# The first expert group's transposes ahead of the fourth half batch's counts, the third group's w1 ahead of its rows, and the fourth batch of x loaded in five pieces

## The chip, the cores and the metric

The kernel runs on one core of one Trainium2 chip. The metric is device time in microseconds (us), lower is better; a comparison is made of several timed executions of each kernel on the same chip. One execution is also recorded by the hardware profiler, and all rows below are from that one.

## What is computed

The input is a batch of 8 sequences of 2496 rows and 256 columns. The reference takes a two-dimensional Fourier transform of each, keeps the real part, and sends the 19968 rows that result through a mixture of 8 experts, one expert per row:

```python
X = np.fft.fft(x, axis=1)
X = np.fft.fft(X, axis=2)
x = X.real.reshape(B * S, D)            # 19968 x 256
logits = x @ w_gate                     # 256 x 8
expert_idx = np.argmax(logits, axis=1)
gate_w = softmax(logits)[arange, expert_idx]
h = np.maximum(xe @ w1[e], 0.0)         # rows of expert e, 256 -> 1024
out[mask] = gate_w[mask, None] * (h @ w2[e])   # 1024 -> 256
```

## The kernel before

**Two halves that overlap.** The transform goes in 16 half batches, called units: the even and the odd part (par 0 and 1) of each of the 8 batches. For one unit VectorE (DVE) folds the loaded x (`fold_w`, `fold_fg`, `fold_z`, `fold_h`, lines 474 to 505), TensorE (PE) multiplies along the sequence (L356, in two quarters q = 0 and 1) and along the columns (`along_d`, L682 to L691), and `route_a` and `route_b` (L529 to L631) find each row's expert, count the rows of each expert (two small matmuls against a triangle and ones, L586 and L587, the *counts*), and scatter the rows by POOL's indirect DMA into a table in DRAM named `bucket` (L617), sorted by expert. The numbers of the rows (L527) are put beside the data by POOL.

**Groups.** The experts' half takes rows from `bucket` in groups. The first 12 groups are of 256 rows of one expert. Which expert and which rows a group has is not known ahead: `first_row` makes a table for the first two groups once units 0 and 1 are counted, and `group_rows` with `table_row` (L923, L1012) makes the next table, for the groups from the third on, once units 0 to 3 are. SP (the engine that issues loads) copies a table into a row, `row<-tab` (L918 and L1022), and reads registers from it (`reg`, L1039). For each group SP loads the rows (`load_rows`, `xr`, L1053), and w1 and w2 of the expert in four pieces each (`load_w`, L1084). A load of rows waits until the scatters of the units that its table covers have landed.

**One group.** PE transposes the rows (`xpose`, L1100), ACT writes a rounded copy `xh` (L1106) and DVE the rest `xl` (L1107). Each w1 piece is split likewise into `wah` (ACT, L1120) and `wal` (DVE, L1121), each w2 piece into the two halves of `wb` (L1135, L1136). For each of four pieces p the first GEMM is 12 matmuls of 256 columns (L1154 to L1156); ACT's relu makes `hh` (L1159) and DVE the rest `hl` (L1160); the second GEMM is 12 matmuls (L1187 to L1190) that read `hh`, `hl` and `wb`, placed two pieces behind the first (`LAG = 2`). `put` scales and writes the result (L1208 to L1211).

**What sets the order.** Inside `start()` (units 0 to 3) the order on PE, DVE and ACT is that of the code (`manual_schedule`). After it a scheduler orders each engine's instructions by its own estimates, beginning from the order in which the code emits them: the main loop takes `next(todo)` for a step of the transform and `next(moe)` for a step of the experts, in a ratio set by `THIRD` and `LEAD`. SP takes its loads in the order in which they are emitted (`after("sp")`), so an instruction that waits holds back all that stand behind it. The PSUM tiles `psH` (4 buffers) are shared by both halves. `load_x(3)` loads batch 3 in two halves of 1.3 MB, `x` having two buffers, so that it waits until PE has read batch 1.

Of the kernel before, what the change touches and what calls it, by code (L numbers as in the profile page):

```python
# [33 lines left out]
WARM = 18  # L34
EARLY = 2
LEAD = 4
THIRD = 26
THREE = 7
FIRST = 8
FSTEPS, AHEAD = 28, 6  # L40
AHEAD_IDS = 3
# [15 lines left out]
SURE = PAIRED + len(ENDING)  # L57
# [151 lines left out]
def fft2_then_moe(ctx: ExitStack, tc: tile.TileContext, i: dict, out: bass.AP):  # L209
# [33 lines left out]
    def load_x(b):  # L243
        x = ff.tile([P, 4, 5, 256], F32, name="x")
        src = i["xin"][b]
        for h in range(2):
            with after("sp"):
                ins = nc.sync.dma_start(out=x[:, 2 * h : 2 * h + 2], in_=src[:, 2 * h : 2 * h + 2])
        xs_of[b] = x
        ch["sp"] = ins.ins  # L250

    slots = ((0, 2), (2, 4), (4, 5))

# [220 lines left out]
    def fold_w(b, sl):  # L474

        x, s = xs_of[b], slice(*sl)
        ch["w"] = nc.vector.tensor_add(x[:, 0::2, s], x[:, 0::2, s], x[:, 1::2, s])
        yield

    def fold_fg(b, sl):  # L480
# [48 lines left out]
    def route_a(b, par, rb, st, fine=False):  # L529
# [44 lines left out]

        if not fine:
            gate()
        if 2 * b + par >= AHEAD_IDS:
            put_ids(rb, b, par)
        st["lg"], st["ohf"], st["ohb"], st["rest"] = lg3, ohf, ohb, (gate, mirror)
        yield  # L580

    def route_b(b, par, rb, st, fine=False):
# [59 lines left out]
    def fft_steps():  # L642
# [88 lines left out]
        def start():  # L731
# [77 lines left out]
            pc()  # L809
            run(tab)  # L810
            qc()
            fb = chain(fold_z(1, 1), fold_batch(2))
            next(fb)
            for _ in along_d(2, (0, 2, 4)):
# [15 lines left out]
                next(fb)  # L830
            st, rb = {}, cols.pop(3)
            run(route_a(1, 1, rb, st, True))
            rb3 = route_b(1, 1, rb, st, True)
            next(rb3)
            next(fb)
            run(rb3)
            return fb

        with ordered():
            fb = start()  # L840
        ch["done"] = 2
        yield
        load_x(3)
        yield
        _, w, g0, count = cuts()[1]
        for _ in group_rows(w, g0, count):
            yield
            next(fb, None)
            yield
        ch["row", 4] = table_row()  # L850
        yield
# [3 lines left out]
        for u, (b, par) in enumerate(units):  # L855
            if u < 4:
                continue
            if par == 0 and 2 < b < B - 1:
                load_x(b + 1)
            three = par and u >= THREE  # L860
            for q in range(2):
                if three:
                    ch["z", u, q] = split_odd(b, q)
                    yield
                if u == THREE - 1:
                    odd_table(1 - q)
                along_s(u, q)
                yield
                if q == 0 and late is not None:
                    yield from late  # L870
            if par == 0:
                yield from fold_z(b, 1)
            elif b + 1 < B:
                yield from fold_batch(b + 1)
            yield from along_d(u)
            late = route(u)
            if u + 1 in [n for n, _, _ in SEGS]:
                yield from late
                late = None
                ch["done"] = u + 1  # L880
# [204 lines left out]
        ch["sp"] = ins.ins  # L1085

    def xpose(g, part):

        xr, n = ch[g]["xr"], tall[g]
        if n < 4 and part:  # L1090
# [6 lines left out]
        for q in range(0 if blocked(g) else 4 if n > 1 else 2):  # L1097
            k, a = (part, q) if n == 4 else divmod(q, n)
            c = (T1, T2)[k]
            nc.tensor.transpose(out=hp[:, q * P : (q + 1) * P], in_=xr[:, a, c : c + P], identity=ident)  # L1100
        if n == 1:
            ch[g]["x"] = mo.tile([P, D], F32, name="ys", bufs=4)
            hi = lo = nc.scalar.copy(ch[g]["x"], hp[:, 0 : 2 * P]).ins
        else:
            xh, xl = (v[:, part] for v in ch[g]["x"])
            hi = nc.scalar.copy(xh, hp).ins  # L1106
            lo = nc.vector.tensor_sub(xl, hp, xh.bitcast(F32)).ins  # L1107
        if part == 0 and not blocked(g):
            gt = mo.tile([P, 4, 2], F32, name="gt", bufs=8)
            with tc.issue_after(hi):  # L1110
                nc.scalar.copy(gt[:, 0:n, 0], xr[:, 0:n, GATE])
            with tc.issue_after(lo):
                nc.vector.tensor_copy(gt[:, 0:n, 1].bitcast(I32), xr[:, 0:n, TID].bitcast(I32))
            ch[g, "gt"] = gt

    def split(src, name):
        hi = mo.tile([P, 512], F32R, name=name + "h")
# [105 lines left out]
    def moe_steps(g0, g1):  # L1223
# [9 lines left out]
        if g0 == 0:  # L1233
            load_rows(g0)
            yield g0
        for part in range(2):
            xpose(g0, part)
        if tall[g0] > 1:
            split1(g0, 0)
        for n in range(len(units) + LAG):  # L1240
            if n < len(units):
                g, p, fs = units[n]
                more, half = g + 1 < g1, tall[g] == 1
                if p == 0 and fs[0] == 0 and more:
                    load_rows(g + 1)
                    w_regs(g + 1)
                    if not half:
                        load_w(g + 1, w1r, "w1", 0)
                if p < 3 and fs[0] == 0 and not half:
                    split1(g, p + 1)  # L1250
                    if more:
                        load_w(g + 1, w1r, "w1", p + 1)
                elif p == 3 and more and not half:
                    xpose(g + 1, fs[0])
                    if fs == (0, 1):
# [29 lines left out]
    for n in sorted({s[0] for s in segs}):  # L1285
        todo = fft_until(n)
        if moe is not None:
# [3 lines left out]
            nm = sum(4 * tall[g] for g in span)  # L1291
            if ch["at"] == 0:
                nf = THIRD
                next(moe)
                for _ in range(LEAD):
                    next(todo, None)
                nf -= LEAD
# [21 lines left out]
        for g in have:  # L1319
            rows_of[g] = row, n  # L1320
        if moe is None:
            moe, ch["at"] = moe_steps(0, SURE), 0
    for _ in moe:
        pass
    total = nc.values_load(row[0:1, 3:4], min_val=0, max_val=KINDS.count("H"))
# [24 lines left out]
```

## Time and profile before

| what | value |
|---|---|
| timed executions, median of 3 | 1188.2 us (1183.52 to 1189.18) |
| the profiled execution | 1166.6 us, of which 1164.5 us are the span from first to last instruction |
| mean granted TensorE clock over the span | 0.968 of full speed |
| busy share of the span | PE 93%, DVE 70%, ACT 52%, POOL 30% |

The profiled execution is 1.8% below the median of the timed ones. Times in the rows count from the start of the span. PE's clock has two levels, shown as 1.00 (2.4 GHz) and 0.50 (1.2 GHz). "Idle before" an instruction is put down to the one that ended the wait; "issue" means that the profile shows nothing that it waited for, "remote" that a semaphore came which the profile can't put to an instruction.

### The profile page before, as it was taken

The page shows a single profiled execution, that of the slowest core. Times are in us where ns is not written, and L with a number is a line of the kernel's source. Part 1 is how long each engine was busy: PE and PEld are TensorE (multiplying, and loading weights), DVE is VectorE, ACT ScalarE, POOL GpSimd, SP SyncE. Part 2 cuts the span into 40 slices and gives each one's busy share as a digit, 9 for nine tenths or more (in the row PEclk, how much of TensorE's full clock was granted, in tenths as well). Part 3 has the DMA queues.
Part 4 walks back from the last instruction along what each step waited for, and adds up shares of the span by engine and source line. Part 5 has one row for each costly group of instructions (what it writes and reads, how often), then busy time and mean ns, then how long its engine had stood idle before and what let it go on. Part 6 is the DMA issues. An engine that isn't in the chain of part 4 may idle for free.

```text
span 1164.5 us, 21457 instructions
## 1 busy us (share of the span) xinstructions
PE 1085.4 (93%) x6229; PEld 926.0 (80%) x6229; DVE 820.5 (70%) x1810; ACT 601.2 (52%) x1375; POOL 353.7 (30%) x348
## 2 busy tenths in 40 slices
PE   8759999999897998997988999999999999999996
PEld 4548998998676787786766888888888888899995
DVE  7678877966887878574666666666666665667774
ACT  2245575765444555353443545555555555556664
POOL 1744524524445142424424112111211211211111
PEclk9979998999998999898989999999999999999999
DMA  9665676557473574451524434453343413455510
GB/s 353 218 229 174 206 244 197 162 142 255 105 223 132 130 228 123 134 133 67 133 59 124 131 64 118 110 129 70 102 115 64 113 38 55 155 157 192 172 47 26
DMA packets 202485, 163.88 MB, mean 141 GB/s; under 512 B 148786, under 2 KB 151827, under 8 KB 200440
## 3 DMA queue, kind: packets, MB, share of 16 engines
q1 hardware_dynamic: 186292, 116.84, 37.7%
q0 software_dynamic: 15776, 45.43, 10.2%
q8 instruction: 51, 0.84, 0.3%
q14 instruction: 74, 0.61, 0.2%
q10 hardware_dynamic: 292, 0.17, 0.1%
HBM read 162.21 MB, written 44.94 MB: 178 GB/s over the span
## 4 chain that ended last, share of the span: by engine, by line
PE 83%; issue 6%; DVE 5%; DMA 2%; another core or an unknown queue 2%; ACT 2%; SPq 0%; POOL 0%; POOLq 0%; DVEq 0%; ACTq 0%
PE psY L1197 21%; PE psH L1154 12%; PE psH L1155 12%; PE psH L1156 12%; PE psY L1198 10%; PE psH L356 2%; PE psY L1187 2%; PE psY L1190 2%; PE psY L1189 2%; PE psH L691 2%; PE psH L690 1%; DMA x<-xin 1%; PE psH L401 1%; PE psH L1100 1%
## 5 line engine op out<-in xcount | busy, mean ns | idle before, releaser
L1197 PE MATMUL psY<-wb,hh 128*128 128x512 f32 x1088 | 405.3, 405 | 15.9 <-DVE ys L1210 12.8
L1211 POOL DMA_INDIRECT out<-ys,gt x160 | 173.6, 1085 | 565.9 <-DVE ys L1210 465.2
L1198 PE MATMUL psY<-wb,hl 128*128 128x256 f32 x1088 | 307.5, 283 | 0.5 <-DVE hl L1160 0.5
L1154 PE MATMUL psH<-xh,wah 128*128 128x512 f32 (+1 forms) x784 | 283.6, 362 | 5.0 <-issue 3.4
L1155 PE MATMUL psH<-xl,wah 128*128 128x512 f32 (+1 forms) x784 | 278.3, 355 | 3.1 <-DVE wb L1136 1.2
L1156 PE MATMUL psH<-xh,wal 128*128 128x512 f32 (+1 forms) x784 | 275.3, 351 | 0.9 <-issue 0.9
L1160 DVE SCALAR_TENSOR_TENSOR hl<-psH,hh 128x512 fp32r<-128x512 f32 (+1 forms) x328 | 220.9, 673 | 60.8 <-ACT hh L1159 47.2
L1197 PEld LDWEIGHTS psY<-wb,hh 128*128 128x128 f32 x1088 | 207.1, 190 | 68.6 <-DVE ys L1210 14.8
L1159 ACT ACTIVATE hh<-psH 128x512 fp32r<-128x512 f32 (+1 forms) x328 | 192.3, 586 | 69.6 <-PE psH L1156 51.7
L1120 ACT CAST wah<-w1r 128x512 fp32r<-128x512 f32 x196 | 121.8, 622 | 205.3 <-PE psH L1155 153.6
L1121 DVE TENSOR_TENSOR wal<-w1r,wah 128x512 fp32r<-128x512 f32 x196 | 135.3, 690 | 130.1 <-ACT wah L1120 92.8
L617 POOL DMA_INDIRECT bucket<-rb,di x160 | 172.0, 1075 | 150.6 <-issue 69.0
L1198 PEld LDWEIGHTS psY<-wb,hl 128*128 128x128 f32 x1088 | 207.7, 191 | 9.7 <-DVE hl L1160 1.5
L1136 DVE TENSOR_TENSOR wb<-w2r,wb 128x512 fp32r<-128x512 f32 x212 | 145.4, 686 | 53.2 <-ACT wb L1135 28.3
L1135 ACT CAST wb<-w2r 128x512 fp32r<-128x512 f32 x212 | 132.5, 625 | 85.1 <-PE psY L1198 48.5
L1154 PEld LDWEIGHTS psH<-xh,wah 128*128 128x128 f32 x784 | 151.3, 193 | 31.7 <-issue 7.6
L1156 PEld LDWEIGHTS psH<-xh,wal 128*128 128x128 f32 x784 | 151.5, 193 | 23.1 <-issue 2.4
L1155 PEld LDWEIGHTS psH<-xl,wah 128*128 128x128 f32 x784 | 151.4, 193 | 13.7 <-issue 2.1
L1208 ACT ACTIVATE ys<-psY,gt 128x256 f32<-128x256 f32 x160 | 65.4, 478 | 12.9 <-PE psY L1190 4.7
L1106 ACT CAST xh<-psH 128x512 fp32r<-128x512 f32 x78 | 45.9, 588 | 44.9 <-DVE psH L1096 42.6
L1107 DVE TENSOR_TENSOR xl<-psH,xh 128x512 fp32r<-128x512 f32 x78 | 53.6, 688 | 14.7 <-ACT xh L1106 13.1
L1210 DVE SCALAR_TENSOR_TENSOR ys<-psY,gt,ys 128x256 f32<-128x256 f32 x136 | 57.5, 476 | 5.4 <-ACT ys L1208 2.7
(217 smaller groups left out, 1108.2 us busy)
## 6 DMA issues: line engine op xcount, KB each, us to landing
w1r<-w SPq DMA_DIRECT2D x212, 256.0 KB
w2r<-w SPq DMA_DIRECT2D x212, 256.0 KB
x<-xin SPq DMA_DIRECT2D x12, 1280.0 KB
xr<-bucket SPq DMA_DIRECT2D x232, 64.0 KB
xr<-bucket SPq DMA_DIRECT2D x20, 266.0 KB
x<-xin SPq DMA_DIRECT2D x3, 1024.0 KB
bucket<-rb,di POOLq DMA_INDIRECT x160
out<-ys,gt POOLq DMA_INDIRECT x160
```

What stands on the lines that cost most here:

```text
L617: ins = nc.gpsimd.indirect_dma_start(out=bucket[:, :], out_offset=IndirectOffsetOnAxis(ap=di[:, n : n + 1].bitcast(U32), axis=0), in_=rb[: ...
L1121: nc.vector.tensor_sub(lo, src, hi.bitcast(F32))
L1135: nc.scalar.copy(wb[:, :, 0], src)
L1136: nc.vector.tensor_sub(wb[:, :, 1], src, wb[:, :, 0].bitcast(F32))
L1154: nc.tensor.matmul(o, lhsT=wh[:, c], rhs=xh[:, k, :], start=(k == 0), stop=False)
L1155: nc.tensor.matmul(o, lhsT=wh[:, c], rhs=xl[:, k, :], start=False, stop=False)
L1156: nc.tensor.matmul(o, lhsT=wl[:, c], rhs=xh[:, k, :], start=False, stop=(k == 1))
L1159: nc.scalar.activation(hh[:, z], hp[:, z], AF.Relu)
L1160: nc.vector.scalar_tensor_tensor(out=hl[:, z], in0=hp[:, z], scalar=0.0, in1=hh[:, z].bitcast(F32), op0=ALU.max, op1=ALU.subtract)
L1197: nc.tensor.matmul(y, lhsT=hh[:, c], rhs=wide_w, start=(first and q == 0), stop=end, skip_group_check=True)
L1198: nc.tensor.matmul(y[:, 0:D], lhsT=hl[:, c], rhs=wb[:, f, 0], start=False, stop=end, skip_group_check=True)
L1211: ins = nc.gpsimd.indirect_dma_start(out=out, out_offset=IndirectOffsetOnAxis(ap=gt[:, a, 1:2].bitcast(U32), axis=0), in_=ys, in_offset=No ...
```

## The change

Four edits, all in the stretch from about 70 to 115 us of the span. The first group's `xpose` becomes a generator `xparts` with stops after the transposes, after `xh` and after the rest, and `start()` takes its steps among those of unit 3's routing: the transposes stand ahead of the counts on PE, `xh` ahead of the copy `mirror` on ACT, and POOL's numbers (`put_ids`) of that unit move behind the scan. `load_x(3)` is replaced by `load_pieces(3)`, five loads of a fifth each (0.5 MB), emitted along with the steps of the second table. The folds of batch 3 (`fold_w`) are kept behind the second table on DVE (`after("tab")`). For the third group, the first whose rows are told by the second table, `load_rows` moves from ahead of w1 to behind its third piece. `THIRD` falls from 26 to 25, since the step that was `load_x(3)` is gone, and a `next(moe)` ahead of the main loop moves into `start()`.

```diff
-THIRD = 26
+THIRD = 25
...
+    def load_pieces(b):
+        for n in range(5):
+            with after("sp"):
+                ch["sp"] = load_slots(b, (n, n + 1)).ins
+            yield
...
-        ch["w"] = nc.vector.tensor_add(x[:, 0::2, s], x[:, 0::2, s], x[:, 1::2, s])
+        with after("tab") if b == 3 else nullcontext():
+            ch["w"] = nc.vector.tensor_add(x[:, 0::2, s], x[:, 0::2, s], x[:, 1::2, s])
...
             run(tab)
             qc()
+            for g in range(g0, g0 + count):
+                rows_of[g] = ch["row", 2], 2
+            moe = ch["moe"] = moe_steps(0, SURE)
+            next(moe)
...
             run(route_a(1, 1, rb, st, True))
+            next(moe)
             rb3 = route_b(1, 1, rb, st, True)
             next(rb3)
+            next(moe)
+            next(rb3)
+            next(moe)
+            run(rb3)
             next(fb)
-            run(rb3)
             return fb
...
-        load_x(3)
-        yield
         _, w, g0, count = cuts()[1]
-        for _ in group_rows(w, g0, count):
+        x3 = load_pieces(3)
+        for n, _ in enumerate(group_rows(w, g0, count)):
             yield
             next(fb, None)
+            if n:
+                next(x3, None)
             yield
...
+            yield from xparts(g0, 0)
+        else:
+            for part in range(2):
+                xpose(g0, part)
...
+                fresh = more and rows_of[g + 1][1] == 4 > rows_of[g][1]
                 if p == 0 and fs[0] == 0 and more:
-                    load_rows(g + 1)
+                    if not fresh:
+                        load_rows(g + 1)
+                    else:
+                        ch[g + 1] = {}
                     w_regs(g + 1)
...
                     if more:
                         load_w(g + 1, w1r, "w1", p + 1)
+                        if fresh and p == 1:
+                            load_rows(g + 1)
...
                 nf = THIRD
-                next(moe)
```

**On PE, behind unit 3's `along_d`.** Before, in the order of the program (L586 and L587 are the counts, L1100 the first group's transposes, L1154 and on its first GEMM):

```order
L683 MATMUL psH<-pack,qc 128x136
L586 LDWEIGHTS trib
L586 MATMUL psH<-ohb,trib 128x80
L587 LDWEIGHTS ones
L587 MATMUL psH<-ohb,ones 128x80
L1100 MATMUL psH<-pack,xr 128x128 x4
L1154 MATMUL psH<-xh,wah 128x256 x2
```

and of the change, whose lines have moved (L1127 are the transposes, L598 and L599 the counts, L1184 and on the first GEMM):

```order
L695 MATMUL psH<-pack,qc 128x136
L1127 MATMUL psH<-pack,xr 128x128 x4
L598 LDWEIGHTS trib
L598 MATMUL psH<-ohb,trib 128x80
L599 LDWEIGHTS ones
L599 MATMUL psH<-ohb,ones 128x80
L1184 MATMUL psH<-xh,wah 128x256
```

The four transposes have gone ahead of the counts.

**On PE, where the first group's second GEMM begins.** Before (psH_1036 is the first GEMM's second piece, psY0 the second GEMM's result, hh_994 the relu of the first piece):

```order
L1155 MATMUL psH_1036<-xl_931,wah_976 128x256
L1156 MATMUL psH_1036<-xh_930,wal_977 128x256
L1154 MATMUL psH_1036<-xh_930,wah_976 128x256
L1155 MATMUL psH_1036<-xl_931,wah_976 128x256
L1156 MATMUL psH_1036<-xh_930,wal_977 128x256
L1187 MATMUL psY0_1092<-wb_1066,hh_994 128x256
L1189 MATMUL psY0_1092<-wb_1066,hh_994 128x256
L1190 MATMUL psY0_1092<-wb_1066,hl_995 128x256
```

and of the change (psH_986 is the first GEMM's first piece, hh_999 and hl_1000 are what ACT and DVE make of it, L1217 to L1220 the second GEMM):

```order
L1184 MATMUL psH_986<-xh_861,wah_947 128x256
L1185 MATMUL psH_986<-xl_862,wah_947 128x256
L1186 MATMUL psH_986<-xh_861,wal_948 128x256
L1217 MATMUL psY0_1095<-wb_1069,hh_999 128x256
L1219 MATMUL psY0_1095<-wb_1069,hh_999 128x256
L1220 MATMUL psY0_1095<-wb_1069,hl_1000 128x256
```

The second piece's 12 matmuls no longer stand between the first piece and the second GEMM that reads it; they now stand behind the transform's 6 rows of L356 (L362 in the change). Ahead of these stood 24 matmuls of the first GEMM and 8 of the second; now 12 and 12.

**On SP, where the third group's loads begin.** Before, behind the second table (`row` is the table's row, xr the group's rows, w1r_126 to w1r_129 the pieces of w1):

```order
L1041 TENSOR_LOAD row
L1041 ISA x2
L1053 ISA
L1053 DMA xr<-bucket 128x532
L1041 TENSOR_LOAD row
L1041 ISA x2
L1041 TENSOR_LOAD row
L1041 ISA x2
L1084 ISA
L1084 DMA w1r_126<-w 128x512
L1084 ISA
L1084 DMA w1r_127<-w 128x512
```

and of the change, from the first w1 piece on:

```order
L1107 DMA w1r_126<-w 128x512
L1107 ISA
L1107 DMA w1r_127<-w 128x512
L1107 ISA
L1107 DMA w2r_133<-w 128x512
L1107 ISA
L1107 DMA w1r_128<-w 128x512
L1064 TENSOR_LOAD row
L1064 ISA x2
L1076 ISA
L1076 DMA xr<-bucket 128x532
```

The rows' load now stands behind three pieces of w1 and one of w2. On DVE the table's last instruction (L1018 before, L1041 in the change) stands ahead of an eviction pair (L416, L419), of one `hl` and of one `wal` that it stood behind, and behind one `wb` that it stood ahead of.

## Rows read from the trace of the kernel before

**Rows 1.** The page's part 4, the chain that ended last, by engine.

```profile
PE 83%; issue 6%; DVE 5%; DMA 2%; another core or an unknown queue 2%; ACT 2%; SPq 0%; POOL 0%; POOLq 0%; DVEq 0%; ACTq 0%
```

**Rows 2.** Busy time by stretch: stretch, length, PE, PEld, DVE, ACT, POOL, clock, DMA.

```profile
70.40:80.60 10.20, 4.50 (x35) 3.88 (x34) 7.15 (x23) 4.54 (x20) 8.02 (x8) 1.00 0.90 324
80.60:87.50 6.90, 6.22 (x28) 5.60 (x28) 6.03 (x21) 2.79 (x7) 3.07 (x4) 0.51 0.55 209
87.50:101.10 13.60, 12.34 (x92) 10.75 (x92) 8.29 (x33) 4.49 (x10) 8.91 (x9) 1.00 0.57 173
101.10:104.50 3.40, 3.40 (x19) 3.40 (x18) 3.00 (x5) 2.61 (x6) 0.00 (x0) 0.50 0.49 151
104.50:140.00 35.50, 34.59 (x262) 31.54 (x262) 34.06 (x79) 21.86 (x57) 13.35 (x11) 1.00 0.64 192
```

**Rows 3.** PE in order of time: start, duration, line, operation, idle before it.

```profile
80.59 0.21 PE L586 MATMUL psH<-ohb,trib 128*128 128x80 bf16 x1 [5.10 <-issue]
82.46 0.79 PE L1154 MATMUL psH<-xh,wah 128*128 128x256 f32 x2 [0.68 <-issue]
...
84.20 0.41 PE L1156 MATMUL psH<-xh,wal 128*128 128x256 f32 x1
84.42 0.41 PE L1154 MATMUL psH<-xh,wah 128*128 128x256 f32 x1
...
88.63 0.28 PE L1189 MATMUL psY<-wb,hh 128*128 128x256 f32 x1
88.75 0.69 PE L356 MATMUL psH<-cs,x 128*128 128x156 f32 x4
...
90.63 0.39 PE L1154 MATMUL psH<-xh,wah 128*128 128x256 f32 x1
...
112.05 0.60 PE L1100 MATMUL psH<-pack,xr 128*128 128x128 f32 x4
```

**Rows 4.** ACT in order of time.

```profile
77.92 0.37 ACT L685 ACTIVATE rb<-psH,g1t 128x128 f32<-128x128 f32 x1 [1.73 <-remote]
...
80.90 0.23 ACT L590 COPY sb<-psH 128x80 f32<-128x80 f32 x1 [0.15 <-issue]
81.82 0.59 ACT L1106 CAST xh<-psH 128x512 fp32r<-128x512 f32 x1 [0.69 <-issue]
...
85.72 0.62 ACT L1120 CAST wah<-w1r 128x512 fp32r<-128x512 f32 x1 [2.60 <-PE psH L1155]
86.25 0.59 ACT L1159 ACTIVATE hh<-psH 128x512 fp32r<-128x512 f32 x1
...
100.36 0.62 ACT L1120 CAST wah<-w1r 128x512 fp32r<-128x512 f32 x1 [5.87 <-issue]
```

**Rows 5.** DVE in order of time.

```profile
82.44 0.69 DVE L1107 TENSOR_TENSOR xl<-psH,xh 128x512 fp32r<-128x512 f32 x1
...
86.87 0.69 DVE L1160 SCALAR_TENSOR_TENSOR hl<-psH,hh 128x512 fp32r<-128x512 f32 x1 [0.83 <-ACT hh L1159]
...
87.55 0.69 DVE L505 TENSOR_TENSOR x<-x 128x512 f32<-128x512 f32 x1
...
92.84 0.15 DVE L1018 TENSOR_TENSOR tab<-tacc 128x1 int32<-128x1 f32 x1
...
107.04 0.68 DVE L1121 TENSOR_TENSOR wal<-w1r,wah 128x512 fp32r<-128x512 f32 x1
```

**Rows 6.** SP: its longest wait (total, times, longest), and two loads in time.

```profile
SPq L1022 <- DVE tab L1018: 16.6, 1, 16.6
...
102.47 0.33 SPq L1053 DMA_DIRECT2D xr<-bucket  x1
104.33 1.03 SPq L1084 DMA_DIRECT2D w1r<-w  x2
```

**Rows 7.** DMA packets in 2 to 6 us (x in 1 KB runs) and 72 to 75 us.

```profile
DMA packets 1354, 1.24 MB, mean 311 GB/s; under 512 B 216, under 2 KB 1341, under 8 KB 1354
DMA packets 107, 0.94 MB, mean 314 GB/s; under 512 B 15, under 2 KB 15, under 8 KB 15
```

More of the change, by code (lines that the diff above doesn't have):

```diff
@@ L576, in route_a, with number @@
             gate()
-        if 2 * b + par >= AHEAD_IDS:
-            put_ids(rb, b, par)
-        st["lg"], st["ohf"], st["ohb"], st["rest"] = lg3, ohf, ohb, (gate, mirror)
+        def number():
+            if 2 * b + par >= AHEAD_IDS:
+                put_ids(rb, b, par)
+        if not fine:
+            number()
+        st["lg"], st["ohf"], st["ohb"], st["rest"] = lg3, ohf, ohb, (gate, mirror, number)
         yield
@@ L867, in fft_steps @@
                 along_s(u, q)
+                next(x3, None)
                 yield
@@ L873, in fft_steps @@
             elif b + 1 < B:
+                run(x3)
                 yield from fold_batch(b + 1)
@@ L1087, in xpose, with xparts @@
     def xpose(g, part):
+        for _ in xparts(g, part):
+            pass
+    def xparts(g, part):
         xr, n = ch[g]["xr"], tall[g]
@@ L1100, in xpose @@
             nc.tensor.transpose(out=hp[:, q * P : (q + 1) * P], in_=xr[:, a, c : c + P], identity=ident)
+        yield
         if n == 1:
@@ L1106, in xpose @@
             hi = nc.scalar.copy(xh, hp).ins
+            yield
             lo = nc.vector.tensor_sub(xl, hp, xh.bitcast(F32)).ins
@@ L1114, in xpose @@
             ch[g, "gt"] = gt
+        yield
     def split(src, name):
@@ L1235, in moe_steps @@
             yield g0
-        for part in range(2):
-            xpose(g0, part)
+            yield from xparts(g0, 0)
+        else:
+            for part in range(2):
+                xpose(g0, part)
         if tall[g0] > 1:
@@ L1321, in fft2_then_moe @@
         if moe is None:
-            moe, ch["at"] = moe_steps(0, SURE), 0
+            moe, ch["at"] = ch["moe"], 0
     for _ in moe:
```

## The prediction

> **What bounds the kernel now.** I read the chain of work that ended last first: 83% of it is PE [rows 1], so a microsecond that PE loses and nothing gives back lasts to the end. The busy time by stretch then tells where PE is not full in the part that the change touches [rows 2]. From 70.4 to 80.6 us PE is busy 4.50 of 10.20; from 104.5 to 140 it is busy 34.59 of 35.5, with DVE at 34.06. Between these lie 24 us in which things can be won: PE restarts at 80.59 behind an idle time of 5.10 [rows 3], runs at the lower clock (0.51) until 87.5, idles 13.60 - 12.34 = 1.26 us before 101.1, and pays with another 3.4 us at 0.50 [rows 2]. PE in order of time shows what the clock does to the first GEMM: from one 256-column matmul to the next 84.42 - 84.20 = 0.21 us at the lower clock, 88.75 - 88.63 = 0.12 at the higher [rows 3]. ACT, DVE and SP in order of time tell who is late: SP stands 16.6 us behind the copy of the second table, which DVE ends at 92.84 + 0.15 [rows 5, 6], and ACT stands 5.87 us until 100.36 for something that the profile doesn't show [rows 4].
>
> The sum is made against the profiled execution, 1166.6 us. The timed executions (median 1188.2) are 1.8% longer, and I carry the difference over as it is. They spread by 0.48%, so about 0.5% is what a measurement of this kernel can tell from no change.
>
> **A. The first group's transposes ahead of the counts.** They now run in PE's idle time before 80.59. On ACT nothing stands between the copy of the counts, which ends at 80.90 + 0.23 = 81.13, and `xh`, which starts at 81.82 because the transposes had still to come [rows 4]. `xh` can start at 81.13, and the first GEMM 0.69 earlier: **-0.7 us**. It can't be more, since the order keeps `xh` behind that copy; if `xl` on DVE (82.44 [rows 5]) doesn't come forward with it, it is nothing.
>
> **B. The second GEMM moved against the first.** The order shows the first GEMM's second piece behind the transform's L356, and the second GEMM directly behind the first piece that it reads. So PE has nothing to do while ACT and DVE make `hh` and `hl`. ACT's `wah` reuses the buffer that the first piece reads and stands ahead of `hh`: from the start of one to the end of the other 86.25 + 0.59 - 85.72 = 1.12 us [rows 4]. Two matmuls of the second GEMM need `hh` alone (0.42); the third needs `hl`, 0.69 on DVE [rows 5]: 0.27 more. The hole is 1.4 us. The first piece starts at 81.8 and ends 12 x 0.21 later, about 84.7 with its wait for `xl`; the hole and ten more matmuls at 0.21 bring PE to L356 at about 88.6. L356 can't come much earlier anyhow: it starts at 88.75 because the fold that it reads runs on DVE until 87.55 + 0.69 = 88.24 [rows 5], and some folds now stand behind the counts, so 88.8. PE thus reaches L356 when it did before, but has 24 matmuls of the group behind it and not 32: 8 x 0.12 = 0.96. A and B together: **+1.0 us** (-0.7 if the hole is filled by a queue that I can't see, +1.5 if the fold comes 0.5 later).
>
> **C. The clock.** It rose at 87.5 after PE had worked on without a stop from 82.46 [rows 2, 3]. With the hole, unbroken work starts at about 86.7, some 4 us later than before, and the rise may come later by as much. The dearest thing in that time is L356, 90.63 - 88.75 = 1.88 at the full clock [rows 3]; twice that is +1.9. At the other end the hole does nothing to a clock that is low already: 0. I take **+1.7**, since the half-rate stretch from 101.1 shows that idle pieces of 1.26 us in all, spread over 13.6, are enough to lower it [rows 2]. The Trainium skill, "TensorE: Matmul & The Clock Gate", section "HAM oscillation", has it that only long idle gaps of PE re-throttle the clock; a hole of B's length would by that leave it alone, and the sum would come out 1.7 lower. The trace disagrees as to the fall at 101.1, where the gaps before were short, and I go by the row.
>
> **D. x in five pieces.** Two pieces go out where two halves did, three behind the next group's w1, so these loads have 1.0 MB ahead of them and not 2.6. Runs of 1 KB move at 311 GB/s at the kernel's start, runs of 10 KB at 314 [rows 7]: the pieces cost nothing as such. Nobody waits for x there: its folds are now behind the table that ended at 92.99, and 2.6 MB at 311 GB/s are 8.4 us, issued from about 71. What hides it is that gap of some 13 us; without it the fold would wait, and L356 of batch 3 behind it. The one thing that lighter traffic may give is ACT's wait of 1.73 before 77.92 [rows 4], on the way to the counts, in a stretch with the DMA engines 0.90 busy [rows 2]. The profile doesn't name its cause, so: 0, with -1.7 as the other end.
>
> **E. The second table earlier.** DVE has an eviction pair, an `hl` and a `wal` less ahead of the table and a `wb` more; at 0.6 to 0.7 each [rows 5] that is about 1.5, and the scan starts some 0.5 earlier, so SP is let go about 2 us sooner. The same five weight loads go out behind it, and the stretch in which ACT stood for 5.87 us and PE idled 1.26 is likely to come again, sooner by up to 2. PE, late by B and C, gets part of that back there. If the hold-up goes altogether, 1.26 of idle and half of the 3.4 at half clock go with it: -3.0. If it comes as before, 0. I take **-2.0**, the lead of the table.
>
> **F. The third group's rows behind w1.** SP is free of the scatters that `xr` waits for, and w1 goes out earlier than 104.33 [rows 6]; but nothing shows that anyone waits for it. The rows were issued at 102.47 and read by PE at 112.05 [rows 3, 6], 9.6 us later. They now stand behind the third w1 piece, which overwrites what DVE splits at 107.04 [rows 5]; without the stand of 5.87 us that is some 3 us sooner. So 107.7 at the latest, plus some 1 us for SP's register loads: 3.3 us before PE needs them. **0**, while that cover lasts; what it costs if it's gone is the third rival. The folds kept behind the table move no work off or onto DVE: 0. POOL's numbers move behind the scan, and the scatters wait for the indices anyway: 0.
>
> **Sum:** +1.0 + 1.7 + 0 - 2.0 + 0 = +0.7 us: 1167.3 in a profiled execution, **1188.9** timed. The forecast is no change that a measurement can tell.
>
> **The rivals.** *First, faster: the hold-up from 93 to 104 goes, and ACT's wait before the counts too.* A -0.7 with B's hole partly filled, D -1.7, E -3.0, and the clock up one stretch earlier, which gives back half of the 3.4 us: -7.1, 1181.1. For it: both waits end on nothing that the rows name and lie in heavy DMA traffic, which the change spreads out. Against it: the same five loads stand behind the same table with the same scatters. The Trainium skill, "DMA: Bandwidth & Descriptors", section "Queues, rings and completion order", says that a DMA engine changes between queues only at packet bounds, so smaller runs let others through sooner; no row here shows that for ACT's wait. Chance 0.19.
>
> *Second: the change does to the end nothing at all,* because what PE loses at 85 us it gets back whole in the hold-up (ACT stands until 100.36 in either case [rows 4]): 1188.2. For it: ACT's wait ended with no PE work that could explain it. Against it: it must end at the same time though the table is earlier. It is inside the forecast's class; chance 0.25.
>
> *Third, slower: the third group's rows come late.* One wait: SP holds `xr` until DVE has split the third w1 piece of the second group, and PE holds the transposes until the rows are there. It decides once the rows land after 112; each microsecond later is one lost, and 5.9 are needed to be told, so a landing at 118, or at about 116.3 with a fall of the clock for one stretch of 3.4 us behind it (1.7). For it: DVE's split came at 107.04, DVE is full from 104.5 on, and the loads ahead fill the same queue. Against it: 3.3 us of cover, and the table 2 us sooner. At 118 the time is 1194.2. Chance 0.14.
>
> The forecast itself has the remaining 0.42, with its own range of 1186 to 1192 from C and E at their ends.
>
> **How the numbers follow.** Faster by over 0.5% is the first rival with a little that it shares: 0.19. Slower by over 0.5% is the third: 0.14. The rest, 0.67, is within 0.5%. For 8 in 10 the range reaches down to the first rival's 1181 and up beyond the third's point, 1195, which also takes in the spread of the timed runs. The likeliest time is 1188.9.
>
> **What would show it right or wrong.** A: transposes before 80 us and `xh` at about 81.1. B: PE idle for 1.1 to 1.4 us between the first piece's last matmul and the second GEMM, at about 85 us. C: the granted clock still 0.50 behind 87.5. D: ACT's 1.73 still there before unit 3's last eviction. E: the table's last instruction at about 91 and not 92.84; ACT's long stand again in the five loads, ended sooner. F: the third group's rows issued at 104 to 109 and PE's transposes of it without a wait. The prediction is wrong if PE's first GEMM of the second group starts more than 6 us from where it did, or if a wait for rows stands ahead of the third group's transposes.

## The result

The changed kernel takes 1186.6 us (median of 22 executions), the kernel before beside it 1179.4 (also 22). The ratio is **1.0055, 95% interval 1.0028 to 1.0082**: 6.5 us slower, 3.3 to 9.7, at the edge of the 0.5% that I called the least that can be told. Two later measurements of the same two kernels, on other chips, gave 1.0010 (0.9983 to 1.0037, experiment 5) and 1.0035 (0.9994 to 1.0076, experiment 9). Weighted by their intervals the three make 1.0033, some 4 us. The ratios leave the disturbed executions out and need not equal the quotient of the medians. The first two of the three don't agree well with each other. The forecast was +0.7 us, no change that can be told, with 1181 to 1195 us as its range. The point 1.0055 lies just beyond the 0.5% at which the prediction speaks of slower, with an interval on both sides of that line; the three together lie within it. On the 1188.2 us that the prediction started from, +6.5 us is 1194.7, at the upper end of its range.

The profiled execution of after took 1191.3 us, its span 1189.4, against 1166.6 and 1164.5 in the profile of before. Most of these 25 us is not the change: single executions of after go from 1172.6 to 1194.2, and of before from 1163.1 to 1189.6 (a few disturbed ones left out), with the mean granted clock from 0.953 to 0.971 in those of after. Between 150 and 1140 us the clock was at its lower level for 71.7 us in this execution and for 27.3 us in that of experiment 5, the same program. What the change does must be read in its stretch, against a marker ahead of it.

The chain that ended last has the same make-up as before [rows 1]:

```profile
PE 83%; issue 6%; DVE 5%; another core or an unknown queue 2%; DMA 2%; ACT 2%; POOL 0%; SPq 0%; POOLq 0%; DVEq 0%; ACTq 0%
```

Busy time by stretch, columns as in [rows 2]; by its rows PE stands still through the whole second row, and the third, at the lower clock, is 11.1 us long where before it was 6.9:

```profile
70.50:81.30 10.80, 6.88 (x46) 5.37 (x45) 8.01 (x24) 5.73 (x19) 6.32 (x7) 1.00 0.64 201
81.30:87.30 6.00, 0.00 (x0) 0.00 (x0) 2.44 (x11) 1.21 (x6) 3.78 (x4) 0.50 1.00 325
87.30:98.40 11.10, 8.92 (x36) 7.60 (x35) 9.80 (x44) 3.50 (x9) 6.06 (x6) 0.50 0.30 109
98.40:102.00 3.60, 3.60 (x28) 3.17 (x29) 2.59 (x5) 1.41 (x3) 2.69 (x4) 1.00 0.60 150
102.00:110.00 8.00, 8.00 (x63) 7.30 (x62) 6.45 (x11) 4.71 (x11) 3.16 (x3) 1.00 0.77 238
110.00:140.00 30.00, 29.52 (x236) 27.97 (x235) 30.00 (x72) 20.54 (x55) 8.67 (x7) 1.00 0.58 179
```

PE in order of time. The transposes (L1127) now run ahead of the counts (L598); the idle time before the counts is 8.41 us and not 5.10 [rows 3]; the second GEMM (L1217) stands directly behind the first piece, with a hole of 0.99; and the third group's transposes wait for nothing:

```profile
78.13 0.40 PE L695 MATMUL psH<-pack,qc 128*128 128x136 f32 x2
78.36 0.60 PE L1127 MATMUL psH<-pack,xr 128*128 128x128 f32 x4
87.38 0.23 PE L598 MATMUL psH<-ohb,trib 128*128 128x80 bf16 x1 [8.41 <-issue]
...
88.47 0.58 PE L1184 MATMUL psH<-xh,wah 128*128 128x256 f32 x1 [0.80 <-ACT xh L1134]
...
93.08 0.58 PE L1217 MATMUL psY<-wb,hh 128*128 128x256 f32 x1 [0.99 <-ACT hh L1189]
...
96.10 1.24 PE L362 MATMUL psH<-cs,x 128*128 128x156 f32 x4
...
117.97 0.60 PE L1127 MATMUL psH<-pack,xr 128*128 128x128 f32 x4
```

ACT in order of time, to be held against [rows 4]. `xh` now follows the copy of the counts at once, as step A had it. But the eviction at 84.72, the last of the fourth half batch, waits for PE's matmuls at 78.13, which end at 78.13 + 0.40 = 78.53: it starts 6.19 us later. The stand of 5.87 us before a `wah` is gone; between 93 and 115 us the longest is 1.43:

```profile
80.39 0.31 ACT L705 ACTIVATE pl<-psH,g1t 128x64 f32<-128x64 f32 x1 [2.18 <-PE psH L1127]
...
84.72 0.37 ACT L697 ACTIVATE rb<-psH,g1t 128x128 f32<-128x128 f32 x1 [3.85 <-remote]
...
87.71 0.23 ACT L602 COPY sb<-psH 128x80 f32<-128x80 f32 x1 [0.17 <-PE psH L599]
87.83 0.59 ACT L1134 CAST xh<-psH 128x512 fp32r<-128x512 f32 x1
...
92.43 0.59 ACT L1189 ACTIVATE hh<-psH 128x512 fp32r<-128x512 f32 x1
...
106.41 0.62 ACT L1150 CAST wah<-w1r 128x512 fp32r<-128x512 f32 x1 [1.43 <-issue]
```

DVE ends the second table at 97.72 + 0.15:

```profile
97.72 0.15 DVE L1041 TENSOR_TENSOR tab<-tacc 128x1 int32<-128x1 f32 x1
```

SP, to be held against [rows 6]: the table's row goes out at 97.90 and the third group's rows at 113.55, 4.4 us before PE reads them at 117.97:

```profile
97.90 0.55 SPq L1045 DMA_DIRECT2D row<-tab  x1
...
113.55 0.33 SPq L1076 DMA_DIRECT2D xr<-bucket  x1
```

**A marker.** POOL's scatters, ten for each half batch, give marks that both kernels have: the first of unit 2 (ahead of all that the change moves), of unit 3 and of unit 4. POOL in order of time, after:

```profile
73.15 1.10 POOL L629 DMA_INDIRECT bucket<-rb,di  x1 [15.52 <-ACT wah L1150]
...
91.32 1.28 POOL L629 DMA_INDIRECT bucket<-rb,di  x1 [1.82 <-DVE end L966]
...
136.82 1.55 POOL L629 DMA_INDIRECT bucket<-rb,di  x1 [1.35 <-issue]
```

From unit 2's first scatter it is 91.32 - 73.15 = 18.17 us to unit 3's and 63.67 to unit 4's. The same worked out for every trace stands behind the experiments.

### The profile page after: what moved, and what is told of

Its sections match the earlier page's. It is cut to its first block, busy times and chain, and to the rows that moved or that the text cites. A ratio compares the mean times of both kernels' runs of the same rounds, so it can differ in the third digit from the quotient of the medians.

```text
span 1189.4 us, 21461 instructions
## 1 busy us (share of the span) xinstructions
PE 1097.7 (92%) x6228; PEld 936.6 (79%) x6229; DVE 820.5 (69%) x1810; ACT 600.7 (51%) x1375; POOL 351.5 (30%) x348
## 4 chain that ended last, share of the span: by engine, by line
PE 83%; issue 6%; DVE 5%; another core or an unknown queue 2%; DMA 2%; ACT 2%; POOL 0%; SPq 0%; POOLq 0%; DVEq 0%; ACTq 0%
PE psY L1227 20%; PE psH L1184 12%; PE psH L1186 12%; PE psH L1185 12%; PE psY L1228 10%; PE psH L362 2%; PE psY L1217 2%; PE psY L1220 2%; PE psY L1219 2%; PE psH L407 2%; PE psH L702 1%; PE psH L703 1%; DMA x<-xin 1%; PE psH L1182 1%
## 5 line engine op out<-in xcount | busy, mean ns | idle before, releaser
L1241 POOL DMA_INDIRECT out<-ys,gt x160 | 171.2, 1070 | 579.4 <-DVE ys L1240 471.9
L1184 PE MATMUL psH<-xh,wah 128*128 128x512 f32 (+1 forms) x784 | 282.8, 361 | 7.7 <-issue 6.2
L1186 PE MATMUL psH<-xh,wal 128*128 128x512 f32 (+1 forms) x784 | 278.4, 355 | 1.4 <-issue 1.4
L1184 PEld LDWEIGHTS psH<-xh,wah 128*128 128x128 f32 x784 | 151.7, 194 | 33.5 <-issue 10.3
```

What stands on the lines that cost most here:

```text
L1184: nc.tensor.matmul(o, lhsT=wh[:, c], rhs=xh[:, k, :], start=(k == 0), stop=False)
L1186: nc.tensor.matmul(o, lhsT=wl[:, c], rhs=xh[:, k, :], start=False, stop=(k == 1))
L1241: ins = nc.gpsimd.indirect_dma_start(out=out, out_offset=IndirectOffsetOnAxis(ap=gt[:, a, 1:2].bitcast(U32), axis=0), in_=ys, in_offset=No ...
```

## The experiments

Experiments 1 to 4 ran on one chip, on which the kernel before took 1087.9 us (23 executions), 5 to 8 on a second (1164.8, 29 executions), 9 to 12 on a third (1177.7, 35 executions). The ratio of each run is to the kernel before on its own chip. The first of these chips differs in kind: its traces show a mean granted clock of 0.992 to 0.994, and of 0.959 to 0.972 on the others.

**1. The order put back.** All of the change, with

```
-LEAD = 4
+LEAD = 3
```

On PE the first GEMM's second piece stands ahead of the second GEMM again, as it did before the change.

> Everything of the change stays; only LEAD is 3 and not 4, which puts the first GEMM's second piece ahead of the second GEMM again, as before the change. Theory 1 (the loss is the second GEMM standing directly behind the piece that it reads: the hole of 1.4 us and the clock that rises some 5 us later): the loss of 6.5 us goes, the ratio to before is 0.998 to 1.001, and in the trace PE goes from the first piece to the second without an idle time over 0.3 us. Theory 2 (the loads: x in five pieces and rows behind w1 disturb the traffic): the ratio stays at 1.004 to 1.008. Theory 3 (the loss has no one place; it is the clock's falls over the whole time): somewhere between, with falls of the clock at other places than 80 to 100 us.

Measured: 1083.4 us, ratio 0.9965 (0.9952 to 0.9977). This is the fastest kernel of the study on this chip, 3.8 us (2.5 to 5.2) ahead of the one before. Whether the changed kernel itself loses here was not measured.

**2. The order alone.** The kernel before, with

```
-LEAD = 4
+LEAD = 5
```

> The kernel before with LEAD 5 and not 4: nothing of the change but the order, the second GEMM directly behind the first piece. Theory 1: the ratio is 1.004 to 1.007, and PE idles 1.1 to 1.4 us between the two and runs at the lower clock to 91 us or later. Theory 2: 0.999 to 1.001. Theory 3: 1.000 to 1.003.

Measured: 1088.5 us, ratio 1.0009 (1.0001 to 1.0018), so 1.0 us (0.1 to 2.0). PE in order of time shows the hole, 1.91 us here:

```profile
75.49 0.58 PE L1187 MATMUL psY<-wb,hh 128*128 128x256 f32 x1 [1.91 <-ACT hh L1159]
```

Theory 1, that the whole loss is this order, falls on this chip: the hole is real, but with the late clock and all that follows it costs 1.0 us, less than the 1.7 that step B gave the hole and the 1.7 that step C gave the clock, and not 6 us.

**3. The transposes alone.** The change to the start, with x of the fourth batch in two halves, its folds not tied and the rows ahead of w1:

```
-        x3 = load_pieces(3)
+        load_x(3)
...
-        with after("tab") if b == 3 else nullcontext():
...
```

> The first group's transposes ahead of the counts, and with them the numbers behind the scan and the order that this gives DVE; x in two halves, the rows ahead of w1 as before, and the first GEMM's second piece ahead of the second GEMM as before. Theory 1: 0.998 to 1.000 (term A, -0.7 us, and at most a little of E). Theory 2: the same. Theory 3, or a loss in DVE's new order (the folds of the third batch behind the route of unit 3): 1.002 to 1.006.

Measured: 1092.7 us, ratio 1.0045 (1.0032 to 1.0058). DVE in order of time names the price: a fold (L483) has come to stand ahead of the table and of `hl`, and x is not there yet:

```profile
69.77 0.16 DVE L950 TENSOR_SCALAR ni<-ni 128x8 int32<-128x8 int32 x1
74.28 1.23 DVE L483 TENSOR_TENSOR x<-x 128x1024 f32<-128x1024 f32 x1 [4.35 <-DMA x<-xin]
...
77.01 0.68 DVE L1186 SCALAR_TENSOR_TENSOR hl<-psH,hh 128x512 fp32r<-128x512 f32 x1
```

PE then waits 3.77 us for that `hl`. So the tie of the folds is what the moved transposes need: the cover that step D named, and the price when it is gone, which no row of before showed (4.9 us for all of this experiment). Experiment 11, with the halves and the tie, has no such wait.

**4. The pieces alone.** The kernel before with five pieces of x and the tied folds; PE, ACT and DVE keep their order:

```
-        load_x(3)
+        x3 = load_pieces(3)
...
+        with after("tab") if b == 3 else nullcontext():
...
```

> The kernel before with x of the 4th batch in five pieces and its folds behind the second table; PE, ACT and DVE have the same order as before, SP alone differs. Theory 1: 0.999 to 1.001, with ACT's wait before unit 3's last eviction at about 1.7 us as it was. Theory 2: 1.003 to 1.006, with a longer idle time on ACT or PE between 70 and 105 us. If the lighter traffic helps (term D's other end): 0.998.

Measured: 1086.4 us, ratio 0.9986 (0.9977 to 0.9996): a gain of 1.5 us (0.4 to 2.5). It didn't come from ACT's wait, which is 0.27 us in all four traces of this chip:

```profile
65.70 0.37 ACT L692 ACTIVATE rb<-psH,g1t 128x128 f32<-128x128 f32 x1 [0.27 <-PE psH L690]
...
97.62 0.62 ACT L1131 CAST wah<-w1r 128x512 fp32r<-128x512 f32 x1 [2.86 <-DMA w1r<-w]
```

The second row names what the long stands of ACT at this place can be: w1 of the second group not yet landed. Where the gain comes from this trace does not settle.

**5 and 6. The two kernels once more,** word for word.

> The changed kernel once more, word for word, beside runs in which the clock seldom falls. If the loss of 0.55% lies in the changed stretch itself (the hole and the late clock, theory 1), the ratio to before is 1.004 to 1.007 here too. If it comes from falls of the clock that the first measurement had in every run (theory 3), then the order's price is what the second experiment has, some 1 us, on top of the gain that the first has, and the ratio is 0.996 to 0.999.

> The kernel before, word for word, for its trace beside those of the other runs: a span of 1084 to 1089 us, and between 90 and 106 us the hold-up in which SP issues five weight loads and PE idles, as it stands in the run with the pieces alone (2 us of idle and 3.4 us at the lower clock).

Measured: 1166.6 us after, ratio 1.0010 (0.9983 to 1.0037); the single execution of the one before took 1163.9. ACT's last eviction again, after (first) and before (second), each with the PE matmuls that it waits for:

```profile
78.51 0.40 PE L695 MATMUL psH<-pack,qc 128*128 128x136 f32 x2
78.75 0.60 PE L1127 MATMUL psH<-pack,xr 128*128 128x128 f32 x4
87.65 0.23 PE L598 MATMUL psH<-ohb,trib 128*128 128x80 bf16 x1 [8.31 <-issue]
```

```profile
84.98 0.37 ACT L697 ACTIVATE rb<-psH,g1t 128x128 f32<-128x128 f32 x1 [5.22 <-remote]
```

```profile
78.77 0.40 PE L683 MATMUL psH<-pack,qc 128*128 128x136 f32 x2
84.33 0.23 PE L586 MATMUL psH<-ohb,trib 128*128 128x80 bf16 x1 [5.17 <-issue]
```

```profile
81.66 0.37 ACT L685 ACTIVATE rb<-psH,g1t 128x128 f32<-128x128 f32 x1 [1.71 <-remote]
```

From the end of the matmuls to ACT's start it is 6.08 us after and 2.49 before.

Both expectations miss. The chip was another one (spans of 1164.5 and 1161.9 us), the ratio lies between those of the two theories, and experiment 6, the kernel before word for word, doesn't have the hold-up that its first trace has between 87.5 and 104.5 us [rows 2]: PE is busy 11.20 of 11.20 us up to 101.1, ACT's longest stand before a `wah` there is 1.66 us, and the clock stays at its higher level. Columns as in [rows 2]:

```profile
89.90:101.10 11.20, 11.20 (x86) 9.97 (x85) 9.02 (x34) 5.74 (x12) 8.77 (x9) 1.00 0.38 119
101.10:104.50 3.40, 3.07 (x24) 2.72 (x23) 1.19 (x2) 0.47 (x1) 1.74 (x2) 1.00 0.96 320
```

**7. w1 ahead of the rows alone,** in the kernel before:

```
-                    load_rows(g + 1)
+                    if not fresh:
+                        load_rows(g + 1)
...
+                        if fresh and p == 1:
+                            load_rows(g + 1)
```

> The kernel before with only the third group's rows behind its third w1 piece; PE, ACT and DVE have the same order as before. If the gain of the first experiment comes from w1 ahead of rows, since SP then no longer holds the five loads behind the scatters that the rows wait for: 0.996 to 0.998, and no idle time of PE over 0.3 us between 92 and 106. If it comes from the transposes and the earlier table: 0.999 to 1.001. If the rows come late, as my third rival had it: over 1.003.

Measured: 1166.5 us, ratio 1.0012 (0.9981 to 1.0043): no difference that can be told. The rows do come late here, by little:

```profile
115.69 0.63 PE L1100 MATMUL psH<-pack,xr 128*128 128x128 f32 x4 [1.14 <-DMA xr<-bucket]
```

**8. The change without w1 ahead of the rows,** the last edit undone.

> The changed kernel with the third group's rows ahead of w1 as they were before; PE, ACT and DVE have the order of the change. If w1 ahead of rows carries the gain: 0.3 to 0.5% above the changed kernel of the same call. If it does nothing by itself: within 0.1% of it.

Measured: 1165.3 us, ratio 0.9992 (0.9960 to 1.0024), 1.3 us below the changed kernel of the same chip, inside both intervals. With experiment 7: no effect that can be told, as step F's 0 had it.

**9. The changed kernel a third time.**

> The changed kernel word for word, as the one that the other three of this call are measured against. Where ACT has its unnamed wait before unit 3's last eviction (1.7 us in the three traces with x in halves, 2.7 to 5.2 in the changed kernel's two and in the one without w1): 1.001 to 1.006 of before. Where ACT has no such wait (0.27 us in all four traces of the first call): 0.997 to 0.999, the gain of the first experiment less the order's 0.1%.

Measured: 1186.1 us, ratio 1.0035 (0.9994 to 1.0076). ACT's wait before the last eviction is there (3.21 us behind PE's matmuls), and ACT's copy of the counts waits for PE once more:

```profile
89.20 0.23 ACT L602 COPY sb<-psH 128x80 f32<-128x80 f32 x1 [1.53 <-PE psH L599]
```

**10. The order put back, a second time** (as experiment 1).

> The first experiment once more, beside the changed kernel. Theory 1 (the order costs most): 0.4 to 0.6% below the changed kernel of this call. Theory 4 (the order costs some 1 us, as the second experiment had it, and the rest is ACT's unnamed wait, which the change lengthens): 0.1 to 0.2% below it, and ACT's wait as long as in the changed kernel.

Measured: 1180.2 us, ratio 1.0041 (1.0007 to 1.0075). By the ratio this is not better than the changed kernel, by the median it is 5.9 us below it, so these executions don't decide between theories 1 and 4. The same program that was 0.35% ahead of before on the first chip is 0.41% behind on this one. ACT in order of time has both waits, the one before the last eviction and one for w1 of the second group:

```profile
84.80 0.37 ACT L697 ACTIVATE rb<-psH,g1t 128x128 f32<-128x128 f32 x1 [5.49 <-remote]
...
103.24 0.62 ACT L1150 CAST wah<-w1r 128x512 fp32r<-128x512 f32 x1 [4.04 <-DMA w1r<-w]
```

**11. As 10, with x in two halves;** `THIRD` is 26 again, since `load_x(3)` is a step again, and in the traces SP alone differs.

```
-THIRD = 25
+THIRD = 26
...
-        x3 = load_pieces(3)
+        load_x(3)
+        yield
...
```

> The tenth kernel with one difference, on SP alone: x of the 4th batch in two halves ahead of the rows and not in five pieces; the folds stay behind the second table. Theory 4a (the three late pieces, issued at about 80 us in the two traces of the changed kernel, keep the traffic heavy, and that lengthens ACT's wait): ACT's wait is back at about 1.7 us, and the kernel 0.1 to 0.4% below the tenth. Theory 4b (the transposes lengthen it): ACT's wait as in the tenth, the times the same within 0.1%. Where there is no such wait at all: within 0.1% of the tenth, since no fold waits for x; this also tells the fold's wait for x of 4.35 us, which the third experiment had, from the transposes: with the folds behind the table it is gone.

Measured: 1184.3 us, ratio 1.0036 (0.9996 to 1.0076). Theory 4a falls, by this one trace: ACT's wait stays long without the late pieces. ACT in order of time, again with a long stand before a `wah`, whose releaser the row doesn't name:

```profile
83.84 0.37 ACT L697 ACTIVATE rb<-psH,g1t 128x128 f32<-128x128 f32 x1 [3.83 <-remote]
...
104.98 0.62 ACT L1147 CAST wah<-w1r 128x512 fp32r<-128x512 f32 x1 [6.09 <-remote]
```

In this kernel the four transposes are the one instruction group that stands elsewhere than before on any engine up to that eviction (PE, ACT, DVE, SP and POOL alike).

**12. As 10, with the rows ahead of w1.**

> The tenth kernel with the third group's rows ahead of w1, as before the change; PE, ACT and DVE have the same order as the tenth. If w1 ahead of rows carries part of the gain of the first experiment: 0.1 to 0.3% above the tenth. If F is nothing, as the prediction had it, and as the seventh and eighth runs have it: within 0.1%.

Measured: 1182.0 us, ratio 1.0018 (0.9978 to 1.0058); against the tenth nothing that can be told.

**The marks of all traces.** From unit 2's first scatter to unit 3's and to unit 4's (us), and "signal": from the end of PE's last matmul of the fourth half batch to the start of ACT's eviction that waits for it. All are worked out from the starts and ends of those instructions as shown above for after. "Result" stands for the traces of the result, whose chip the record doesn't name: it may be one of the others.

| trace | chip | signal | to unit 3 | to unit 4 |
|---|---|---|---|---|
| before; its repetition (6); w1 alone (7) | result; 2nd; 2nd | 2.44; 2.49; 1.57 | 16.76; 15.29; 16.41 | 62.56; 59.32; 60.61 |
| after; again (5); third time (9); without w1 (8) | result; 2nd; 3rd; 2nd | 6.19; 6.08; 3.21; 4.00 | 18.17; 18.05; 18.21; 18.15 | 63.67; 63.40; 64.59; 64.54 |
| order back (10); in halves (11); without w1 (12) | 3rd | 6.41; 4.81; 6.18 | 18.40; 18.11; 18.17 | 65.56; 66.71; 66.33 |
| order alone (2); pieces alone (4) | 1st | 0.04; 0.04 | 14.31; 14.04 | 58.78; 58.74 |
| transposes alone (3); order back (1) | 1st | 0.04; 0.04 | 19.33; 13.94 | 62.06; 53.62 |

## Why the prediction was right, and where it was not

Means of the first two rows of the table: to unit 3's scatter 16.15 before and 18.15 after, **+2.0**; from there to unit 4's 44.7 and 45.9, **+1.2**; together +3.2, beside 6.5, 1.2 and 4.1 us in the three timed comparisons. The prediction had -0.7 for the first part (A, with D's 0) and +1.7 + 1.7 - 2.0 = +1.4 for the second (B, C, E). So the first part is off by 2.7 us. The second agrees in its sum, but by luck: +1.2 is a mean of -0.3 on the result's traces and +1.8 on the second chip, and the terms are not what they were taken for (below). Nor do the marks follow the times trace by trace: up to unit 4's scatter the result's two traces differ by 1.1 us where the executions differ by 6.5, and those of the second chip by 4.0 where they differ by 1.2. The marks tell what moved in this stretch; what the timed 6.5 us are made of they don't show.

**A, -0.7: the step that failed.** What it priced is there. From the last eviction to the first GEMM it takes 88.47 - 84.72 = 3.75 us after and 82.46 - 77.92 = 4.54 before [rows 3, 4]: -0.8, and the same 3.8 in experiments 5, 10 and 12. In 8, 9 and 11 it takes 4.3 to 5.1, since there PE's signal for the counts is late too. On the first chip the first GEMM also starts sooner, at 69.57 in experiment 1 and at 70.19 in experiment 4; of these 0.62 us the counts account for 0.26 (68.53 and 68.79), A for 0.36:

```profile
69.57 0.50 PE L1184 MATMUL psH<-xh,wah 128*128 128x256 f32 x2 [0.80 <-ACT xh L1134]
```

```profile
70.19 0.56 PE L1165 MATMUL psH<-xh,wah 128*128 128x256 f32 x2 [0.68 <-ACT xh L1117]
```

What it missed is that "PE's idle time before 80.59" was not free for the transposes: with them behind the last matmul, ACT's wait for that matmul grew. The signal took 1.57 to 2.49 us in three traces with the transposes behind the counts, and 3.21 to 6.41 in seven with them ahead; with x in halves too (4.81), with and without w1 ahead of the rows, in either order of the GEMMs. From PE's last matmul to the first GEMM, with all waits between, it is 6.5 to 7.0 us in the three and 8.3 to 10.2 in the seven. On the chip where the signal takes 0.04 us, the transposes don't lengthen it, and there the kernel with all of the change and the old order is the fastest.

That the change to the start lengthens the wait is borne out by ten traces without overlap, four of them on one chip (1.57 and 2.49 against 4.00 and 6.08). That it is the transposes in it is argued by elimination, from experiment 11 alone, on a chip on which no trace of before was taken; the transposes alone ran only where the signal is on time. What ACT waited for can be told: the semaphore events kept with the traces, which no view prints, have an update of PE's semaphore 0.02 to 0.03 us ahead of ACT's start in all ten, so "remote" was PE. By what mechanism PE's signal is late is not shown. It is late already one block earlier, whose matmuls end ahead of the transposes: ACT's L705 at 80.39 starts 2.79 us behind the end of L703 after, and its counterpart 1.15 behind before.

The Trainium skill, "Perfetto Trace Analysis", section "Tensor Engine Instruction (MATMUL, LD_WEIGHTS)", has it that a matmul's end in a profile is estimated, and that its semaphore goes out only when the writes to PSUM are acknowledged; by that PE may have been held up itself while the rows show it done. The trace agrees in so far as ACT's start lies 6.19 us behind an end that the row puts at 78.53; whether PE or only its signal was held up no run here shows. I had the row (1.73, "remote") in hand and took it as a wait that the change might shorten or leave (D: 0, -1.7); that work put on PE behind it might lengthen it, I did not bound.

**B, a hole of 1.4 us:** 0.99 in after and in experiments 5 and 9; 1.91 on the first chip. With the late clock and all that follows it costs 1.0 us (0.1 to 2.0) on the first chip (experiment 2), where the sum gave the hole 1.7 and the clock another 1.7. On the second chip, where there was no hold-up to give anything back, the second part takes 1.8 us longer in after than in before: about half of the 3.4.

**C, +1.7:** the clock rose at 98.4 and not at 87.5. PE was busy for 8.92 us at the lower clock and not 6.22 [rows 2], so (8.92 - 6.22) / 2 = 1.35 us. Counted from ACT's last eviction, the rise came 98.4 - 84.72 = 13.7 us later in after, 14.8 and 14.9 in experiments 5 and 8, and 8.7 in experiment 9, where it came ahead of the hole; in the six traces of these chips without the hole it was 7.1 to 10.4 (9.6 in before). Experiment 2 has the hole alone: 14.9 us, beside 8.2 and 9.1 in experiments 4 and 1 of the same chip. So the rise comes later with the hole, in four traces of five. The Trainium skill, "TensorE: Matmul & The Clock Gate", section "HAM oscillation", speaks of long gaps that bring the clock down; read as I did, that a hole this short leaves the clock alone, it doesn't hold for a clock that has yet to rise.

**D, 0:** the tie is needed, as it said (experiment 3: 4.35 us of waiting without it). The pieces alone gained 1.5 us on the first chip; on the third, pieces and halves differ by nothing that can be told (1.0041 and 1.0036). ACT's wait of 1.73 was not shortened by them in any trace; the pieces without the transposes ran only on the chip that doesn't have it.

**E, -2.0:** half right. Against the last eviction the table is earlier, as it said: its last instruction starts 92.84 - 77.92 = 14.9 us behind it before and 97.72 - 84.72 = 13.0 after, so -1.9. A's late signal takes that away: against unit 2's first scatter it is 92.84 - 68.56 = 24.3 before and 97.72 - 73.15 = 24.6 after. On the first chip, where the signal is on time, the lead is there against both (18.2 us behind that scatter in experiment 1, 21.2 in experiment 4).

What E gave back came about as well: ACT's stand of 5.87 us is gone, PE is busy 8.00 of 8.00 from 102 to 110, and no fall of the clock follows 98.4 before 150 us. One reason that fits is B's order: PE has the second piece and its second GEMM still to do while w1 of the second group lands, so the stand is covered. None of the five traces with the new order has the hold-up (after and experiments 2, 5, 8 and 9). Of the nine with the old order five have it: before, and experiments 4, 10, 11 and 12, in the last three with ACT standing 4.04 to 6.10 us and PE 2.00 to 4.09. Experiments 1, 3, 6 and 7 don't. Since experiment 6 is the kernel before itself, the hold-up doesn't always come, and E priced it from a single trace. On the third chip, where the order put back has it, the way from unit 3's scatter to unit 4's is 48.0 us, against 46.4 in experiment 9; there the edit that makes the hole may be the one that covers the stand. That is argued, not shown.

**F, 0, and the third rival:** right; the rows were issued 4.4 us before PE read them, and the transposes didn't wait. In experiment 7, without the rest of the change, they did, by 1.14 us: the cover was as thin as feared. The first rival (faster) had the hold-up going, which in the result's traces it did, and ACT's wait before the counts too, which grew. That wait was for PE's signal, so no transfer stood in it; whether heavy traffic delays the signal no run shows. The second rival, no effect at the end, fits experiment 5's 1.0010 and not the result's interval.

**The prediction's own signs.** Of its two signs of being wrong one came up: PE's first GEMM of the second group starts 9.6 us later, before (first) and after (second):

```profile
97.84 0.39 PE L1154 MATMUL psH<-xh,wah 128*128 128x256 f32 x1
```

```profile
107.39 0.39 PE L1184 MATMUL psH<-xh,wah 128*128 128x256 f32 x1
```

Counted from unit 2's first scatter it is 5.0 us, and 7.2 from experiment 6 to 5. That is more than unit 4's scatter moved (1.1 and 4.1): the new order has put the transform's work ahead of the group's, which this sign did not allow for. The other sign, a wait for rows, did not come.

**Open:** what makes PE's signal late, and why not on the first chip; what the timed 6.5 us are made of; where the 1.5 us of the pieces alone come from; and whether the changed kernel itself is faster than before on the first chip, where it was not run.

## What to carry to other kernels

Idle time of an engine is free for moved work only if what ended that idle time is known: here it was a wait with no named releaser, and with four transposes put into it, it was longer. A hole that a new order opens may be the cover of the next stand, so undo it in a run before calling it a loss. Where executions of one program differ by 2% and chips by 8%, measure a stretch between two marks of the same program, one ahead of the change, and take the trace of the kernel before more than once: the hold-up that a term was priced from was not in the second one.

## What was not expected of the hardware

The same program took 1087.9 us on one chip and 1164.8 to 1179.4 on the others. The lower clock is part of it: 14 to 19 us of each trace on the first chip, 67 to 114 us of each on the others. The wait for PE's signal (0.04 us on the one, 1.6 to 6.4 on the others) is another part; unit 2's first scatter, ahead of all that was changed, stands at 59.2 to 60.3 us there and at 68.6 to 74.6 here.
